# A chunk-selecting attention with a gated MLP: a new held order of the work, the first tile's bounds left out, the bias turned in half or full height

## The chip, the cores and the metric

One core of a Trainium2 chip runs the whole program. The metric is the device time of the run in microseconds, as the median of several runs. The engines are named as in the profile: PE is TensorE (its weight loads are PEld), DVE is VectorE, ACT is ScalarE, POOL is GpSimd, SP is SyncE, which here only issues transfers.

## The reference

Four batches of eight heads, 768 positions, head size 64. Each query picks six chunks of 32 keys by an upper bound of its scores, attends to those alone, and the result goes through a gated MLP that also mixes positions.

```python
k_min = np.min(k_chunks, axis=3)
k_max = np.max(k_chunks, axis=3)
ub = np.sum(np.maximum(q[:, :, :, None, :] * k_min[:, :, None, :, :], q[:, :, :, None, :] * k_max[:, :, None, :, :]), axis=-1)
causal = pos[:, None] // chunk >= np.arange(nc)[None, :]
ub = np.where(causal, ub, -1000000000.0)
top_chunks = np.argsort(ub, axis=-1)[..., -top_k:]
scores = scale * np.matmul(q, k.transpose(0, 1, 3, 2))
sel = (j_chunk == top_chunks[..., None]).any(axis=-2)
mask = sel & (pos[:, None] >= pos[None, :])
scores = np.where(mask, scores, -1000000000.0)
...
attn = attn / (np.sum(attn, axis=-1, keepdims=True) + 1e-09)
return np.matmul(attn, v).astype(np.float32)
...
h = np.maximum(x @ w_in, 0.0)
u, v = (h[..., :d_ff // 2], h[..., d_ff // 2:])
v_n = (v - mu) / np.sqrt(var + 1e-06)
v_s = np.einsum('ts,bsd->btd', w_spatial, v_n) + b_spatial[None, :, None]
gated = u * v_s
return (gated @ w_out).astype(np.float32)
```

## The kernel before

**Tiling.** Heads go in pairs: sixteen pairs `p`, four to a batch `b`. The two heads of a pair lie in partitions 0 to 63 and 64 to 127, so that a product over the head size is a matmul of half height (64 rows, "64*128" in the profile), one for each head; products over 128 rows are of full height ("128*128"). The 768 positions are six tiles `i` of 128, with four chunks each.

**Pieces.** `work_list` cuts the work into 1395 named pieces, each with an engine (or a choice of two), a duration that a planner assumes, the pieces that it comes after, and the buffers that it makes and uses. Pieces of one engine run in the order in which they are written out; between engines semaphores hold them back. For a pair they are, in the order of their data:

| piece | engine | what it does | line |
|---|---|---|---|
| load, cast | SP, POOL | q, k, v from memory; to 16 bits | L633, L621, L638 |
| turn, kT, qT, qp | PE or SP; ACT or DVE | q and k transposed; the negative part of q | L652, L617, L688, L690 |
| ext | DVE | largest and smallest key of each chunk | L671 |
| bounds, ub | PE; ACT or DVE | the upper bounds by matmul; copied out of PSUM | L702; L617, L619, L711 |
| top, leave | DVE | the eight largest bounds of tiles 1 to 5; which chunks are left out | L715, L724 |
| pk, mx | PE, DVE | scores of a unit of keys; their maxima by chunk | L732, L735, L786; L807 |
| minus, kept, shift | POOL, POOL, DVE | the maximum over the chunks that are kept | L811, L817, L824 |
| turn_bias, bT | PE, ACT | the 16-bit bias of every query and chunk, transposed by a matmul with the identity | L831, L835 |
| probs, ex, cut | PE, ACT, POOL | scores again with the bias added; exp; the diagonal cut | L856, L863; L871; L877 |
| weigh, av, sum, inv, norm | PE, ACT, DVE, DVE, POOL or DVE | times v, and divided by the sums | L885, L889, L893, L900, L907 |
| turn_x, xT | PE and ACT, or SP | transposed for the MLP | L922, L931 |

For a batch the MLP's pieces are hv, vr, bn, rstd, vn (one half, normalized), hu, uT (the other half), mix (positions mixed), ms, plus, gT (bias, gate), og, oe, od (the last product, its eviction, its store). They start when a batch's four pairs are done; pieces of pairs of the next batch run among them. The first three pairs find their maxima in another way (kd, fd, fr, fi, fb, L795 and L801).

Small constants are made at the start: `ident`, `far`, `rows` (the four instructions L580 to L585 on POOL, after DVE's `clear`) and `member`, which probs needs.

**First tile.** The queries of tile 0 see at most four chunks, so all visible ones are kept: `top` has no piece for tile 0, its threshold is a constant, and a chunk is left out only where the bound is a huge negative number. `bounds` nevertheless computes all of tile 0. For pairs 0 to 5 (`EARLY`) a matmul of `far` with `big` adds this huge negative number to chunks ahead of the query; for later pairs `ub` adds `far32` on VectorE.

**Order.** Two texts hold the plan: `RANK`, a rank for each piece, and `WHERE`, a letter for each of the 96 pieces that have a choice of engine. `order` runs through a model of the five engines in time: whenever an engine is free it begins the ready piece of lowest rank that finds its buffers free, taking the first buffer that is free in the model. The times of that model come from the durations in `work_list`, 0.095 us for a change between half and full height among them (the kinds in `TILED` are of half height), and a delay after each engine's work. The tile buffers in PSUM are called "two" (three of them) and "mg" (two).

Of the kernel before, what the change touches and what calls it, by code (L numbers as in the profile page):

```python
# [16 lines left out]
P = 128  # L17
# [14 lines left out]
RANK = """  # L32
# [51 lines left out]
"""  # L84
WHERE = """
AAAAGAGAGVGVGAAVAGAGAGVVAGAGAGAVVVVVAVAVAAAAAVVAVGGGGVGGAAVAAAAAAAAAAAVVAVAVVAAVAAVVGGGGGVVAAAAA
"""


class Work:  # L90
# [23 lines left out]
    def order(self):  # L114
# [5 lines left out]
        for i, (_, _, _, after, new, old, _) in enumerate(pieces):  # L120
            for b in new + old:
                users[b] = users.get(b, 0) + 1
            for a in after:
                then[self.index[a]].append(i)
                todo[i] += 1
# [27 lines left out]
        def begin(e):  # L153
            nonlocal bus, late, tiled
            aside, found = [], False
            while ready[e] and not found:
                due, i = heapq.heappop(ready[e])
                if begun[i]:
                    continue
# [907 lines left out]
```

## Time and profile before

| | us |
|---|---|
| median of three runs | 249.05 (248.89 to 249.26) |
| the profiled execution, its time | 248.22 |
| its span, first to last instruction | 246.5 |
| TensorE's granted clock | 1.000 |

The view of waits shows who waited for whom (engine and line, what it waited for: us in total, times, longest). The longest ones of PE and DVE:

```profile
PE mg L652 <- DVE k L619: 6.1, 1, 6.1
DVE tmp L1012 <- PE mg L1001: 7.7, 9, 2.0
DVE rc L893 <- ACT av L889: 4.9, 3, 2.2
PE two L856 <- ACT bT L835: 1.9, 3, 0.8
PE two L856 <- DVE cmax L807: 1.9, 3, 1.0
```

A row of a timeline has the start in us from the span's start, the length, the engine, line, operation, what it writes and reads, and the number of instructions merged into the row; in brackets stands the idle time ahead of it and what ended it. A row of a group has the count, the busy time in us, the mean length of one in ns, and the idle time ahead with those who ended it. Neighbouring instructions of one engine overlap by a little in these rows, as the next starts before the last has drained.

### The profile page before, as it was taken

What the parts mean: (1) busy time and instruction counts of PE and PEld (TensorE: products, weight loads), DVE (VectorE), ACT (ScalarE), POOL (GpSimd) and SP (SyncE); (2) the same over time, 40 slices, a digit from 0 to 9 for tenths busy, and PEclk for the clock granted to TensorE, in tenths of its full rate; (3) what the DMA queues carried; (4) which work ended last, traced back from release to release, by engine and by line L of the source; (5) the groups of instructions that cost most, each with busy time, mean ns of one, the idle gap of its engine ahead of it and who ended that gap; (6) DMA issues with size and microseconds to landing.
All of it is one profiled execution on the core that took longest, in us unless ns stands there. A gap on an engine that the chain in (4) does not pass through costs nothing.

```text
span 246.5 us, 9019 instructions
## 1 busy us (share of the span) xinstructions
PE 224.9 (91%) x3780; PEld 144.6 (59%) x3780; DVE 206.5 (84%) x512; ACT 191.9 (78%) x298; POOL 165.9 (67%) x209
## 2 busy tenths in 40 slices
PE   0898778878999999999999999999999999999993
PEld 0656457666755675666665576666745566645551
DVE  4799999999999999799998997899998853349670
ACT  3598887979998999587859897897679969767312
POOL 8879749887785377999965929999926147402160
PEclk9999999999999999999999999999999999999999
DMA  7969996699999949484899997128900010350005
GB/s 189 325 186 201 257 242 127 122 164 241 168 186 235 216 82 187 89 170 112 190 161 271 175 200 125 34 75 140 268 22 19 0 36 0 105 188 0 0 28 227
DMA packets 93895, 35.51 MB, mean 144 GB/s; under 512 B 86208, under 2 KB 90144, under 8 KB 93856
## 3 DMA queue, kind: packets, MB, share of 16 engines
q1 hardware_dynamic: 91568, 31.81, 61.9%
q0 software_dynamic: 2016, 2.75, 6.5%
q8 instruction: 29, 0.48, 0.8%
q10 hardware_dynamic: 272, 0.39, 0.5%
q14 instruction: 10, 0.08, 0.1%
HBM read 24.77 MB, written 6.29 MB: 126 GB/s over the span
## 4 chain that ended last, share of the span: by engine, by line
PE 48%; DVE 28%; ACT 14%; DMA 4%; issue 3%; POOL 2%; DVEq 0%; ACTq 0%
DVE cmax L807 11%; PE mg L1001 11%; ACT pr L871 8%; PE mg L1024 6%; PE mg L885 5%; PE two L856 4%; PE mg L937 3%; PE two L863 3%; DVE stats L954 3%; DVE ext L671 3%; PE two L786 3%; DVE top L715 2%; PE mg L990 2%; DMA k<-in_k_dram 2%; DVE cmax L801 2%
## 5 line engine op out<-in xcount | busy, mean ns | idle before, releaser
L871 ACT ACTIVATE pr<-two 128x1024 f16<-128x1024 f32 (+1 forms) x96 | 85.3, 934 | 5.4 <-PE two L863 4.8
L807 DVE TENSOR_REDUCE cmax<-two 128x24 f32<-128x768 f32 (+4 forms) x104 | 85.3, 843 | 3.5 <-PE two L735 2.0
L856 PE MATMUL two<-qT,kT 64*128 64x128 f16 (+3 forms) x384 | 40.5, 258 | 5.4 <-ACT bT L835 1.9
L863 PE MATMUL two<-bT,member 64*128 64x128 f16 (+1 forms) x512 | 39.7, 233 | 0.0
L877 POOL TENSOR_SCALAR_AFFINE_SELECT pr<-pr 128x768 f16<-128x768 f16 x32 | 27.9, 886 | 9.1 <-ACT pr L871 9.0
L1019 POOL TENSOR_TENSOR vr<-tmp,uT 128x384 f16<-128x384 f32 x27 | 24.5, 922 | 11.9 <-DVE tmp L1012 11.8
L671 DVE TENSOR_REDUCE ext<-kT 128x24 f16<-128x768 f16 x32 | 29.5, 936 | 1.9 <-ACT kT L617 1.7
L1001 PE MATMUL mg<-wsT,vn 128*128 128x384 f16 x168 | 30.2, 327 | 0.0
L856 PEld LDWEIGHTS <-kT 64*128 64x128 f16 x384 | 19.9, 94 | 17.2 <-issue 15.1
L863 PEld LDWEIGHTS <-member 64*128 64x128 f16 x512 | 25.7, 94 | 5.1
L885 PE MATMUL mg<-v,pr 128*128 128x65 f16 x672 | 25.9, 194 | 0.7 <-POOL pr L877 0.5
L786 PE MATMUL two<-kT,qT 64*128 64x384 f16 (+4 forms) x182 | 24.6, 280 | 1.4 <-ACT pr L871 0.5
L885 PEld LDWEIGHTS <-pr 128*128 128x128 f16 x672 | 23.1, 98 | 3.6 <-issue 1.0
L1001 PEld LDWEIGHTS <-vn 128*128 128x128 f16 x192 | 17.7, 98 | 12.2 <-issue 0.6
L990 PE MATMUL mg<-xT,w_in_sb 128*128 128x384 f16 x112 | 22.4, 328 | 0.0
L907 POOL TENSOR_TENSOR x<-av,rc 128x768 f16<-128x768 f32 x11 | 16.2, 1469 | 8.8 <-DVE rc L900 4.9
L732 PE MATMUL two<-kT,qT 64*128 64x128 f16 x192 | 19.6, 221 | 2.3 <-ACT qT L617 1.0
L1024 PE MATMUL mg<-w_out_sb,vr 128*128 128x512 f16 x84 | 20.8, 380 | 0.0
L937 PE MATMUL mg<-w_in_sb,xT 128*128 128x512 f16 x84 | 20.3, 380 | 0.4 <-DVE o L619 0.4
L889 ACT COPY av<-mg 128x390 f32<-128x390 f32 x32 | 15.6, 500 | 6.2 <-PE mg L885 6.0
L954 DVE BATCH_NORM_STATS2 stats<-vr 128x6 f32<-128x512 f32 x24 | 16.6, 692 | 4.0 <-ACT vr L942 2.9
L735 PE MATMUL two<-half_ahead,ident 64*128 64x64 f16 x192 | 19.8, 193 | 0.0
(113 smaller groups left out, 496.8 us busy)
## 6 DMA issues: line engine op xcount, KB each, us to landing
q<-in_q_dram SPq DMA_DIRECT2D x16, 384.0 KB, 6.4
v<-in_v_dram SPq DMA_DIRECT2D x16, 384.0 KB, 5.7
out_dram<-o SPq DMA_DIRECT2D x24, 256.0 KB, 2.1
k<-in_k_dram SPq DMA_DIRECT2D x15, 384.0 KB, 5.7
vr<-in_moe_w_spatial_dram POOLq DMA_DIRECT2D x6, 192.0 KB, 5.6
w_in_sb<-in_moe_w_in_dram POOLq DMA_DIRECT2D x4, 256.0 KB, 8.8
w_out_sb<-in_moe_w_out_dram POOLq DMA_DIRECT2D x4, 128.0 KB, 4.5
k<-in_k_dram ACTq DMA_DIRECT2D x1, 384.0 KB, 4.7
```

The lines of the kernel that those rows point to most:

```text
L671: nc.vector.tensor_reduce(held["ext", p][:, m], src, axis=AX.X, op=Alu.min if m else Alu.max, negate=(m == 1))
L786: mm(t[:, h, o:o + before], lhsT=qT[rows[h], c], rhs=kT[rows[h], a * CH:a * CH + before], start=True, stop=True)
L807: nc.vector.tensor_reduce(tops(p)[:, i // 2, :, i % 2, a:z], held["two", (p, u)][:, :, o:o + n].rearrange("p h (c e) -> p h c e", e=CH), a ...
L856: mm(t[:, h, z:z + n * P], lhsT=kT[rows[h], keys], rhs=qT[rows[h], i * P:(i + n) * P], start=True, stop=False)
L863: mm(d, lhsT=member[rows[h], r, keys], rhs=bT[rows[h], m * P:(m + w_) * P].rearrange("c (m s) -> c m s", s=P), start=False, stop=(n == 1 o ...
L871: nc.scalar.activation(out=held["pr", p][:, :, c0:c0 + n], in_=held["two", (p, "e", c0)][:, :, 0:n], func=Act.Exp, scale=scale)
L877: nc.gpsimd.affine_select(out=d, in_=d, compare_op=Alu.is_ge, fill=0.0, base=0, channel_multiplier=-1, pattern=[[0, NT], [1, P]])
L885: mm(a[:, i, :], lhsT=pr[:, at[t, i]:at[t, i] + P], rhs=vp[:, h * NT + t, :], start=(t == 0), stop=(t == i))
L937: mm(t, lhsT=held["xT", b][:, ko, i * P:(i + 1) * P], rhs=w_in_sb[:, ko, DH:2 * DH], start=(ko == 0), stop=(ko == NDO - 1))
L990: mm(t, lhsT=w_in_sb[:, ko, db * P:(db + 1) * P], rhs=held["xT", b][:, ko, s * HS:(s + 1) * HS], start=(ko == 0), stop=(ko == NDO - 1))
L1001: mm(t, lhsT=held["vn", b][:, si, db * P:(db + 1) * P], rhs=wsT[:, si, s * HS:(s + 1) * HS], start=(si == 0), stop=(si == NT - 1))
L1024: mm(t, lhsT=held["vr", ("g", b)][:, ko, i * P:(i + 1) * P], rhs=w_out_sb[:, ko, :], start=(ko == 0), stop=(ko == KO - 1))
```

## The change

**The order.** `RANK` and `WHERE` are new. `order` no longer runs a model in time: the rank of a piece is its place in the program. A buffer is taken when its last user has been written out, the one first whose last use lies furthest back. The assumed durations of bounds, norm, bn, rstd1, plus and gT are altered; since the order is held, they no longer enter into it.

```diff
-        free = {e: 0.0 for e in self.ENGINES}
-        ready = {e: [] for e in self.ENGINES}
...
-        heapq.heapify(events)
-        while len(result) < n:
...
+        held = {tag: [None] * k for tag, k in self.bufs.items()}
...
+        for (name, on, _, _, _, _, _), at in zip(pieces, rank):
+            result[at] = name, engine[next(where)] if len(on) > 1 else next(iter(on)), at
+        done = set()
+        for at, (name, _, _) in enumerate(result):
+            _, _, _, after, new, old, _ = pieces[self.index[name]]
+            assert all(a in done for a in after) and all(b in slot for b in old), name
+            for b in new:
+                tenants = held[b[0]]
+                free = [(-1 if x is None else last[x], k) for k, x in enumerate(tenants) if x is None or users[x] == 0]
+                assert free, name
+                slot[b] = min(free)[1]
+                tenants[slot[b]] = b
+            for b in new + old:
+                users[b] -= 1
+                last[b] = at
+            done.add(name)
         return result, slot
```

What the new texts say, read piece by piece against the old order (the ranks begin as follows, 1395 of them):

```diff
 RANK = """
-0 9 100 7 13 10 5 1 28 103 118 168 128 124 256 303 296 313 298 327 425 450 446 421 430 435 398 407 417 422 403 411 388
...
 WHERE = """
-AAAAGAGAGVGVGAAVAGAGAGVVAGAGAGAVVVVVAVAVAAAAAVVAVGGGGVGGAAVAAAAAAAAAAAAVVAVAVVAAVAAVVGGGGGVVAAAAA
+VAAAGVGAGAGAGAAVAVAVAGAVAGAVAGAGAVAGAAAAAAAAVAVAGVGGVVVGAAAVAAAAAAAAAAAAVAAVAVVAAAVGGGVGGGVAAAVVA
```

- 34 of the 96 choices go to another engine. To DVE: kT of pair 0, ub 1, norm 6, 7 and 11, four gT, and some of oe, vn and uT; away from it: ub 3 and 4 and qp 9, 14 and 15 to ACT, norm 13 and 15 and three gT to POOL, and some of oe, vn and uT. In numbers DVE has one kT, one norm and one gT more, and three qp, one oe and one ub fewer.
- About half of each engine's pieces change their place against the others. `rows` on POOL stands behind the casts of k and q 1, k 2 and kd 0, and ahead of the cast of q 2. The loads of v come later on SP, those of q 1 and k 1 earlier.
- On PE half and full height alternate 172 times in the old order and 158 times in the new one; up to turn_bias of pair 4, 33 and 37 times.
- On DVE, shift of pair 11 stands behind ext 13, mx 12.6 and 13.0, 13.1, 13.6 and 13.7, the first four top of pair 13, ub 13, and sum, inv and norm of pair 9, all of which came after it. Shift of pairs 8 and 13 moves ahead.
- On POOL both cuts of pair 15 stand ahead of three gT of batch 2. On ACT the last exp of pair 15 stands behind av 14.1. Turn_x of pair 15 stands ahead of the last og of batch 2.

**The first tile's bounds.** Tile 0 has the matmul of `far` with `big` alone, now for every pair; later pairs get `far32` added as well, which leaves a number as far below the limit.

```diff
-            each = [(big, far[:, i])] * (p < EARLY) + [(qT[:, c], x[:, 0]), (qp[:, c], x[:, 0]), (qp[:, c], x[:, 1])]
+            each = [(big, far[:, i])] * (p < EARLY or i == 0) + [(qT[:, c], x[:, 0]), (qp[:, c], x[:, 0]), (qp[:, c], x[:, 1])] * (i > 0)
```

Each matmul is issued for two heads: 48 become 42 for a pair below 6, and 36 become 32 for the others.

**The turned bias.** Where neither neighbour of a turn_bias on PE is of half height (pairs 5, 9, 10 and 15 in the new order), it is turned over all 128 rows, with the half of the identity that picks the wanted columns. The result is the same.

```diff
+    EITHER = ("turn_bias",)
...
+    turned = [name for name, e, _ in order if e == "PE"]
+    whole = {name[1] for a, name, z in zip(turned, turned[1:], turned[2:])
+             if name[0] in Work.EITHER and not (a[0] in Work.TILED or z[0] in Work.TILED)}
...
-                r = slice(g * D, (g + 1) * D)
-                mm(t[:, g, m * D:(m + 1) * D], lhsT=bias[slot["bias", p]][r, 4 * m:4 * m + 4, :].rearrange("p g c -> p (g c)"), rhs=ident[r, r], start=True, stop=True)
+                r, c = slice(g * D, (g + 1) * D), slice(0, P)
+                if p in whole:
+                    r, c = c, r
+                mm(t[:, g, m * D:(m + 1) * D], lhsT=bias[slot["bias", p]][r, 4 * m:4 * m + 4, :].rearrange("p g c -> p (g c)"),
+                   rhs=ident[r, c] if p in whole else ident[r, r], start=True, stop=True)
```

More of the change, by code (lines that the diff above doesn't have):

```diff
@@ L1 @@
-import heapq
 import math
@@ L32 @@
 RANK = """
[51 rows of a table removed]
[51 rows of a table added]
 """
 WHERE = """
-AAAAGAGAGVGVGAAVAGAGAGVVAGAGAGAVVVVVAVAVAAAAAVVAVGGGGVGGAAVAAAAAAAAAAAVVAVAVVAAVAAVVGGGGGVVAAAAA
+VAAAGVGAGAGAGAAVAVAVAGAVAGAVAGAGAVAGAAAAAAAAVAVAGVGGVVVGAAAVAAAAAAAAVAAVAVAAVVAAAVGGGVGGGVAAAVVA
 """
@@ L116, in order @@
         pieces, n = self.pieces, len(self.pieces)
-        users, slot, freed_at, done_at = {}, {}, {}, {}
-        slots = {tag: [None] * k for tag, k in self.bufs.items()}
-        then, todo, ready_at, begun = [[] for _ in range(n)], [0] * n, [0.0] * n, [False] * n
-        for i, (_, _, _, after, new, old, _) in enumerate(pieces):
+        rank, where = [int(x) for x in RANK.split()], iter(WHERE.replace("\n", ""))
+        engine = dict(P="PE", V="DVE", A="ACT", G="POOL", S="SP")
+        assert sorted(rank) == list(range(n))
@@ L121, in order @@
+        users, slot, last, result = {}, {}, {}, [None] * n
+        held = {tag: [None] * k for tag, k in self.bufs.items()}
+        for _, _, _, _, new, old, _ in pieces:
             for b in new + old:
                 users[b] = users.get(b, 0) + 1
-            for a in after:
-                then[self.index[a]].append(i)
-                todo[i] += 1
-        rank, where = [int(x) for x in RANK.split()], iter(WHERE.replace("\n", ""))
-        engine = dict(P="PE", V="DVE", A="ACT", G="POOL", S="SP")
@@ L318, in work_list @@
         far_pe = p < EARLY
-        add("bounds", {"PE": (6 * far_pe + 18) * 0.027},
+        add("bounds", {"PE": 0.54 if far_pe else 0.412},
             DUE["bounds"],
@@ L396, in work_list @@
                 add("inv", {"DVE": 0.14}, at, 0, after=[("sum", p, 0)], old=[("rc", (p, 0))])
-                add("norm", {"POOL": 1.6, "DVE": 1.45}, at, 0, after=[("inv", p, 0)], old=[("av", p), ("rc", (p, 0))], new=[("x", p)])
+                add("norm", {"POOL": 1.5, "DVE": 1.15}, at, 0, after=[("inv", p, 0)], old=[("av", p), ("rc", (p, 0))], new=[("x", p)])
                 continue
```

87 lines of the change are left out of this document (4 added, 83 removed), and 101 rows, old and new, of the table RANK.

## The prediction

> **What bounds the kernel now.** I began with the page's busy times and chain of waits, then cut the span into three stretches.
>
> ```profile
> span 246.5 us, 9019 instructions
> PE 224.9 (91%) x3780; PEld 144.6 (59%) x3780; DVE 206.5 (84%) x512; ACT 191.9 (78%) x298; POOL 165.9 (67%) x209
> PE 48%; DVE 28%; ACT 14%; DMA 4%; issue 3%; POOL 2%; DVEq 0%; ACTq 0%
> ...
> 0.00:60.00 60.00, 44.91 (x1086) 33.23 (x1087) 54.00 (x154) 47.70 (x66) 47.56 (x76) 1.00 0.92 204
> 60.00:180.00 120.00, 118.30 (x2098) 76.44 (x2097) 112.59 (x274) 100.46 (x162) 95.23 (x110) 1.00 0.88 162
> 180.00:246.50 66.50, 61.71 (x599) 34.92 (x597) 39.86 (x87) 43.72 (x72) 23.09 (x24) 1.00 0.17 57
> ```
>
> The window rows give PE, PEld, DVE, ACT and POOL in that order. Up to 60 us PE is idle for 60 − 44.91 = 15.1 us: there VectorE, busy for 54.00 of 60, hands out the work. From 60 to 180 us PE is idle for only 1.7 us, while VectorE is idle for 7.4 us.
>
> ```profile
> 241.88 0.88 PE two L1024 x4
> 242.82 0.59 ACT o L617
> ```
>
> These two rows of the chain of waits show where PE ends: 241.88 + 0.88 = 242.8 us. After it come 3.7 us of eviction and store, so of PE's 4.8 idle us after 180 about 1.1 lie ahead of its end. From 60 us on PE waits about 2.8 us in all. A microsecond of PE work taken out behind 60 us therefore shortens the run, unless PE then waits for something else; taken out ahead of 60 us it only widens a gap.
>
> **The change part by part.** First the prices, in three stretches of PE's timeline (start, length, operation).
>
> ```profile
> 101.96 0.20 PE L702 MATMUL two<-ext,qp 64*128 64x24 f16 x4
> ...
> 102.33 0.20 PE L702 MATMUL two<-ext,qp 64*128 64x24 f16 x4
> ...
> 127.29 1.03 PE L937 MATMUL mg<-w_in_sb,xT 128*128 128x512 f16 x4
> 128.25 0.26 PE L831 MATMUL two<-ident,bias 64*128 64x64 f16 x6
> 128.44 0.39 PE L937 MATMUL mg<-w_in_sb,xT 128*128 128x512 f16 x1
> ...
> 211.87 1.02 PE L1024 MATMUL mg<-w_out_sb,vr 128*128 128x512 f16 x4
> 212.73 0.83 PE L885 MATMUL mg<-v,pr 128*128 128x65 f16 x21
> ```
>
> *First tile's bounds.* Between the two L702 rows lie five tiles of six matmuls: 0.37 us / 30 = 12.3 ns each. The edit drops 6 matmuls for each of pairs 0 to 5 and 4 for each of pairs 6 to 15. The first 36 (0.44 us) mostly fall in the stretch where PE has gaps, so I count them as nothing; without that cover they would be worth 0.44. The other 40 are worth 40 × 12.3 ns = **0.49 us**.
>
> *Changes of height.* From og to weigh, both of full height, the next start lies 211.87 + 1.02 − 212.73 = 0.16 us ahead of the end before it. From hv to the half-height turned bias it lies 127.29 + 1.03 − 128.25 = 0.07 ahead, and back again 128.25 + 0.26 − 128.44 = 0.07. A change of height thus costs about 0.095 us (0.16 − 0.07, at the rows' two digits). Walking PE's pieces in the two held orders I count 172 changes before and 158 after, 8 of those removed by the turned bias in full height. Up to turn_bias of pair 4 (59.7 us in the trace) there are 33 before and 37 after; behind it 139 and 121. Behind it 18 × 0.095 = **1.71 us** go; the four added ahead of it (0.38 us) lie in PE's gaps.
>
> *Turned bias in full height.* This meets pairs 5, 9, 10 and 15. Six half-height matmuls start (0.26 − 0.19) / 5 = 14 ns apart, taking the 0.19 us of one matmul as the last one's length. Its nearest full-height row is weigh: (0.83 − 0.19) / 20 = 32 ns. So the piece grows by 5 × 18 = 0.09 us, four times: **−0.36 us**. Bounds: nothing, if its passes overlapped as before, and 0.36.
>
> The Trainium skill, "TensorEngine Tiling (Array Packing)", speaks on both sides. Its "Key Properties" say that a change of tiling mode drains TensorE, and the 0.095 us at L831 agrees. Its "When to Use Tiling" advises two row tiles for a contraction of 64, up to twice as fast, which this edit gives up. By a plain doubling of the 0.07 us of starts the four would lose an estimated 0.28 instead of 0.36.
>
> So PE's work behind 60 us falls by 0.49 + 1.71 − 0.36 = **1.84 us**. Two small pk pieces also move ahead of turn_bias 4; I count that as nothing, since the early stretch may pay for it.
>
> *The engines of 34 pieces and the moved orders.* VectorE's durations, from the groups of instructions (count, then busy us, mean ns):
>
> ```profile
> L807 DVE TENSOR_REDUCE cmax<-two 128x24 f32<-128x768 f32 (+4 forms) x104 | 85.3, 843 | 3.5 <-PE two L735 2.0 <-PE two L786 1.3
> L671 DVE TENSOR_REDUCE ext<-kT 128x24 f16<-128x768 f16 x32 | 29.5, 936 | 1.9 <-ACT kT L617 1.7
> L907 POOL TENSOR_TENSOR x<-av,rc 128x768 f16<-128x768 f32 x11 | 16.2, 1469 | 8.8 <-DVE rc L900 4.9 <-ACT bT L835 3.3 <-ACT pr L871 0.3
> L907 DVE TENSOR_TENSOR x<-av,rc 128x768 f16<-128x768 f32 x5 | 5.0, 996 | 0.1
> L715 DVE MAX8 top<-ub 128x8 f32<-128x16 f32 (+4 forms) x160 | 14.8, 156 | 0.0
> L711 DVE TENSOR_TENSOR ub<-two,far 128x288 f32<-128x288 f32 x10 | 4.4, 441 | 2.5 <-PE two L702 2.4
> L619 DVE COPY o<-mg 128x512 f32<-128x512 f32 x6 | 4.1, 678 | 3.4 <-PE mg L1024 3.4
> L1019 DVE TENSOR_TENSOR vr<-tmp,uT 128x384 f16<-128x384 f32 x5 | 3.6, 739 | 0.2
> L690 DVE TENSOR_SCALAR qp<-qT 128x768 f16<-128x768 f16 x3 | 1.3, 424 | 0.2 <-DMA qT<-q 0.2
> L619 DVE COPY ub<-two 128x288 f32<-128x288 f32 x2 | 0.9, 446 | 0.0
> ...
> 3.86 0.73 POOL L580 MEMSET member<- 32x768 f16 x1
> ...
> 6.82 0.73 POOL L585 MEMSET member<- 1x768 f16 x1
> ```
>
> VectorE gains one norm (+0.99), one gT (+0.74) and kT 0 (about 0.8, in its idle time ahead of the first ext). It loses three qp (1.27), one oe (0.68) and one ub (0.45). The balance is +0.1, or −0.7 without kT 0: **nothing**, with PE's work as the cover. GpSimd loses a norm and a gT. ScalarE gains the three qp, an oe and a ub and gives up kT 0; at 78% it has room. The moved loads, casts and `rows` go past other pieces of SP's and GpSimd's queues: `rows` (the last two lines, 3.86 to 7.55: 3.7 us at GpSimd's start) now stands ahead of the cast of q 2. GpSimd is idle for 12.4 of the first 60 us, so I take nothing; if the early stretch lacked that cover it could lose up to those 3.7.
>
> *VectorE's waits for GpSimd.* A "leave" (L724), its two group rows, two long ones, and GpSimd beside the second:
>
> ```profile
> L724 DVE SCALAR_TENSOR_TENSOR bias<-top,ub x16: 442/502/1164, 14.0 to 188.4; 128x288 f16<-128x288 f32 x16
> L724 DVE SCALAR_TENSOR_TENSOR bias<-top,ub 128x288 f16<-128x288 f32 x16 | 10.3, 646 | 0.1
> 28.44 1.04 DVE L724 SCALAR_TENSOR_TENSOR bias<-top,ub 128x288 f16<-128x288 f32 x1
> ...
> 40.38 1.06 DVE L724 SCALAR_TENSOR_TENSOR bias<-top,ub 128x288 f16<-128x288 f32 x1
> 39.44 1.68 POOL L877 TENSOR_SCALAR_AFFINE_SELECT pr<-pr 128x768 f16<-128x768 f16 x2
> 41.08 1.04 POOL L638 CAST v<-v 128x768 f16<-128x768 f32 x1
> L638 POOL CAST v<-v 128x768 f16<-128x768 f32 x16 | 13.6, 852 | 0.2
> ```
>
> At 40.38 it takes 1.06 us where the shortest takes 0.44, ending 0.3 us after GpSimd's cut; the next cast then takes 1.04 instead of 0.85. Over 16 the excess is 10.3 − 16 × 0.442 = 3.2 us, the most that a better order could regain here; the other bound is as much again, if the new order meets GpSimd more often. I take zero: where the overlaps fall is set at run time, and PE binds where most of them lie.
>
> The Trainium skill's "SBUF — State Buffer", "Who interferes with whom", says that a VectorE instruction with two SBUF inputs and a GpSimd one that reads SBUF exclude each other for a whole instruction. This case's rows agree. By it a wait avoided on VectorE can reappear on GpSimd, so a full 3.2 us off the sum would be too much.
>
> *New waits.* The turned bias of a pair waits for `shift` (L824), and everything on PE stands behind it.
>
> ```profile
> 147.34 0.45 DVE L824 TENSOR_REDUCE bias<-kept 128x12 f16<-128x288 f32 x1
> 155.89 0.25 PE L831 MATMUL two<-ident,bias 64*128 64x64 f16 x6
> ```
>
> For pair 11 the slack is 155.89 − 147.79 = 8.1 us. In the new order five mx, one ext, four top, norm, sum and inv of pair 9, ub 13, two moved norms and ub 1 come ahead of shift 11, and two oe, one qp and two ub leave. By the means above, with 0.38 for sum and inv, that is 4.2 + 0.9 + 0.6 + 3.0 + 0.4 + 0.9 − 2.7 = 7.3 us. PE meanwhile reaches turn_bias 11 about 0.9 us of work sooner. The slack left is 8.1 − 7.3 − 0.9, about nothing. I charge **+0.4 us** for waits there, between none and the rival below.
>
> *The tail.*
>
> ```profile
> 211.52 2.49 POOL L877 TENSOR_SCALAR_AFFINE_SELECT pr<-pr 128x768 f16<-128x768 f16 x2 [2.65 <-ACT pr L871]
> 214.06 0.84 PE L885 MATMUL mg<-v,pr 128*128 128x65 f16 x21 [0.50 <-POOL pr L877]
> 219.15 0.81 PE L937 MATMUL mg<-w_in_sb,xT 128*128 128x512 f16 x3 [0.45 <-DVE o L619]
> ```
>
> PE waits 0.50 us for pair 15's second cut. The new order makes both cuts before three gT pieces, and weigh 15.0 waits instead for the last exp, which og 2.3 and 2.0 (about 1.7 us) nearly cover: **−0.4 us**. Norm 15 moves to GpSimd (1469 against 996 ns), but turn_x 15 now stands ahead of the last og: the 0.45 us stays.
>
> **Sum.** −1.84 + 0.4 − 0.4 = −1.84. The profiled execution took 248.22 us (its span and 1.72 around it) and would take 246.4. The median of the runs, 249.05, lies 0.83 above it; I forecast **247.2 us**.
>
> **Rivals.**
>
> *VectorE gains too (0.18).* The leaves at 28.44 and 40.38 lose 0.6 us each in the stretch where PE waits for VectorE. Without these waits and without the late ones: 249.05 − 1.84 − 1.2 − 0.4 = 245.6. For it: VectorE's 54.00 of 60. Against: by the means above, shift 3 and 4 now stand behind 0.4 and 1.5 us more VectorE work.
>
> *Late shifts, slower (0.27).* In the stretch 60 to 180 VectorE's 7.4 us of idle grow by 40%, or 3.0 us, because its order is more tightly bound to PE, ScalarE and the three "two" buffers. With no slack at pairs 9 to 11, PE stops for it: 249.05 − 1.84 + 3.0 + 0.2 = 250.4. It decides once VectorE is over 1.84 us later there than planned. Against: at p 8 and 13 shift moves ahead.
>
> *Even (0.13).* The same lateness, about 1.8 us: 249.05. The work goes, and PE waits instead.
>
> **How the numbers follow.** The forecast has 0.42. About 0.2% or 0.5 us separates a change from none, so faster means under 248.55: 0.18 and nearly all of 0.42 give 0.60; same 0.13; slower 0.27. The range 245.3 to 250.3 leaves out the upper half of the slow rival (0.13) and the far third of the first (0.06). The forecast's own range is 246.4 (no late waits, and the early bounds' 0.44 counted) to 248.2 (no gain in the tail, and one more long leave among the early ones, 0.6).
>
> **What would show it.** The bounds should show 76 matmuls fewer. PE's starts across a height change stay 0.095 us dearer. PE idle between 60 us and its end should stay at 2 to 4 us; 5 or more, with turn_bias behind L824, is the slower rival. If L724's mean falls near 450 ns and PE's idle before 60 us under 14 us, the first rival holds. The prediction is wrong if PE's early idle grows by over 1.5 us.

## The result, and the profile after

The changed kernel takes **257.18 us** (median of 4 runs, 256.91 to 258.07) against 249.16 for the kernel before beside it: a ratio of 1.0328, with a 95% interval from 1.0300 to 1.0356. The forecast was 247.2 us with a range from 245.3 to 250.3. Both the sign and the range were wrong.

The page of the changed kernel (its span is 256.4 us), busy times and the shares of its chain of waits; then its windows (PE, PEld, DVE, ACT, POOL busy, granted clock, DMA share, GB/s):

```profile
PE 227.2 (89%) x3704; PEld 147.0 (57%) x3704; DVE 214.5 (84%) x510; ACT 194.9 (76%) x302; POOL 165.2 (64%) x207
DVE 41%; PE 40%; ACT 7%; DMA 6%; POOL 4%; issue 1%; DVEq 0%; ACTq 0%; POOLq 0%
...
0.00:60.00 60.00, 44.35 (x1008) 32.69 (x1008) 54.33 (x150) 45.78 (x64) 45.42 (x74) 0.97 0.89 193
60.00:180.00 120.00, 110.96 (x1909) 72.55 (x1908) 111.59 (x250) 97.23 (x156) 86.26 (x100) 0.96 0.84 147
180.00:256.40 76.40, 71.86 (x797) 41.75 (x793) 48.56 (x112) 51.91 (x83) 33.48 (x34) 1.00 0.35 83
...
60.00:80.00 20.00, 16.75 (x303) 12.09 (x301) 16.10 (x37) 15.24 (x23) 11.04 (x15) 0.91 0.91 147
80.00:100.00 20.00, 15.78 (x289) 10.87 (x286) 19.45 (x38) 15.03 (x26) 9.76 (x13) 0.89 1.20 198
...
20.33:23.72 3.39, 3.39 (x26) 1.79 (x24) 3.39 (x8) 3.07 (x5) 1.86 (x3) 0.50 0.53 122
```

The same two short stretches of the kernel before:

```profile
60.00:80.00 20.00, 19.78 (x310) 12.65 (x308) 19.18 (x42) 18.18 (x29) 14.32 (x19) 1.00 1.20 201
80.00:100.00 20.00, 19.72 (x381) 13.20 (x378) 19.40 (x53) 19.09 (x32) 12.84 (x14) 1.00 0.92 164
```

The span grew by 9.9 us. PE's idle time makes 7.65 of it (29.2 − 21.6): +0.56 before 60 us, **+3.03 from 60 to 80, +3.94 from 80 to 100**, +0.37 from there to 180, −0.25 behind. PE's busy time makes the other 2.25, though it issues 76 matmuls fewer: the granted clock is 0.91 and 0.89 in the same two stretches, 0.94 from 100 to 120 us and 0.50 from 20.3 to 23.7 us, where it was 1.00, so matmuls last longer. The chain of waits, 48% PE and 28% DVE before, is now 40% PE and 41% DVE. So nearly all of the added idle time lies between 60 and 100 us. This is the timeline there, with two later rows of PE (start, length, engine; in brackets what ended the wait):

```profile
61.74 0.40 PE L538 MATMUL mg<-ident,vr 128*128 128x128 f16 x4
63.77 0.23 PE L538 MATMUL mg<-ident,vr 128*128 128x128 f16 x1 [1.64 <-DMA vr<-in_moe_w_spatial_dram]
64.85 0.29 PE L538 MATMUL mg<-ident,vr 128*128 128x128 f16 x1 [0.85 <-DMA vr<-in_moe_w_spatial_dram]
...
91.10 0.58 POOL L533 DMA_DIRECT2D w_out_sb<-in_moe_w_out_dram  x1
91.31 4.36 DVE L905 SCALAR_TENSOR_TENSOR nmr<-mv,rstd 128x6 f32<-128x6 f32 x1
91.69 0.84 POOL L567 CAST v<-v 128x768 f16<-128x768 f32 x1
92.47 0.87 POOL L809 TENSOR_SCALAR_AFFINE_SELECT pr<-pr 128x768 f16<-128x768 f16 x1
93.29 0.82 POOL L567 CAST v<-v 128x768 f16<-128x768 f32 x1
94.06 0.82 POOL L550 CAST q<-q 128x768 f16<-128x768 f32 x1
94.83 0.82 POOL L550 CAST k<-k 128x768 f16<-128x768 f32 x1
97.28 0.20 PE L631 MATMUL two<-far,big 64*128 64x24 f16 x2 [4.22 <-DVE ub L640]
...
136.40 0.35 PE L762 MATMUL two<-ident,bias 128*128 128x64 f16 x6 [0.58 <-DVE cmax L736]
```

Two things are new. Turn_ws (L538) of tile 4 now stands ahead of the weights' arrival, and PE waits 1.64 + 0.85 us for the transfer. And `nmr`, the product of rstd2 (L905), 128 x 6 numbers, takes **4.36 us**: it starts at 91.31 and ends at 95.67, with the last of five instructions that GpSimd runs without a pause (94.83 + 0.82 = 95.65). Everything behind it on VectorE waits, so the `ub` that frees a "two" buffer comes late, and PE stands 4.22 us ahead of bounds 8. In the kernel before the same product met GpSimd's cuts at the same place of its order:

```profile
85.22 1.69 POOL L877 TENSOR_SCALAR_AFFINE_SELECT pr<-pr 128x768 f16<-128x768 f16 x2
85.38 0.72 DVE L973 SCALAR_TENSOR_TENSOR nmr<-mv,rstd 128x6 f32<-128x6 f32 x1
```

There it ended at 86.10, between the two cuts. Two groups of VectorE's instructions that read two operands from SBUF, after:

```profile
L653 DVE SCALAR_TENSOR_TENSOR bias<-top,ub 128x288 f16<-128x288 f32 x16 | 12.0, 763 | 0.0
L905 DVE SCALAR_TENSOR_TENSOR nmr<-mv,rstd 128x6 f32<-128x6 f32 (+1 forms) x5 | 6.1, 1214 | 0.1
```

Before, the leaves took 10.3 us and the five `nmr` 1.3: these are 1.7 and 4.8 us more. The new order meets more of these waits, not fewer.

### The profile page after: what moved, and what is told of

Read it like the earlier page. It is cut to its first block, busy times and chain, and to the rows that moved or that the text cites. A ratio compares the mean times of both kernels' runs of the same rounds, so it can differ in the third digit from the quotient of the medians.

```text
span 256.4 us, 8826 instructions
## 1 busy us (share of the span) xinstructions
PE 227.2 (89%) x3704; PEld 147.0 (57%) x3704; DVE 214.5 (84%) x510; ACT 194.9 (76%) x302; POOL 165.2 (64%) x207
## 4 chain that ended last, share of the span: by engine, by line
DVE 41%; PE 40%; ACT 7%; DMA 6%; POOL 4%; issue 1%; DVEq 0%; ACTq 0%; POOLq 0%
DVE cmax L736 16%; PE mg L933 9%; PE mg L956 5%; DVE ext L600 5%; PE mg L817 5%; DVE stats L886 4%; DMA vr<-in_moe_w_spatial_dram 4%; PE two L788 3%; DVE bias L653 3%; ACT pr L803 3%; PE two L795 3%; DVE top L644 2%; DVE nmr L905 2%; PE two L715 2%; PE mg L922 2%; DMA k<-in_k_dram 2%
## 5 line engine op out<-in xcount | busy, mean ns | idle before, releaser
L736 DVE TENSOR_REDUCE cmax<-two 128x24 f32<-128x768 f32 (+4 forms) x104 | 85.0, 844 | 7.3 <-PE two L664 4.0
L809 POOL TENSOR_SCALAR_AFFINE_SELECT pr<-pr 128x768 f16<-128x768 f16 x32 | 30.1, 948 | 10.9 <-ACT pr L803 10.7
L933 PE MATMUL mg<-wsT,vn 128*128 128x384 f16 x168 | 30.9, 327 | 0.1
L788 PEld LDWEIGHTS <-kT 64*128 64x128 f16 x384 | 19.5, 94 | 16.1 <-issue 13.7
L817 PE MATMUL mg<-v,pr 128*128 128x65 f16 x672 | 27.6, 198 | 0.0
L715 PE MATMUL two<-kT,qT 64*128 64x256 f16 (+4 forms) x182 | 25.6, 287 | 1.9 <-DVE cmax L736 1.4
L817 PEld LDWEIGHTS <-pr 128*128 128x128 f16 x672 | 24.6, 101 | 3.5 <-issue 1.0
L839 POOL TENSOR_TENSOR x<-av,rc 128x768 f16<-128x768 f32 x10 | 14.7, 1472 | 16.2 <-DVE rc L832 14.9
L661 PE MATMUL two<-kT,qT 64*128 64x128 f16 x192 | 20.2, 225 | 2.3 <-ACT qT L546 0.9
L922 PE MATMUL mg<-xT,w_in_sb 128*128 128x384 f16 x112 | 21.8, 327 | 0.2
L664 PE MATMUL two<-half_ahead,ident 64*128 64x64 f16 x192 | 20.4, 195 | 0.0
L869 PE MATMUL mg<-w_in_sb,xT 128*128 128x512 f16 x84 | 20.3, 380 | 0.0
L912 ACT ACTIVATE vn<-vr,nmr,rstd 128x512 f16<-128x512 f32 x21 | 16.4, 811 | 5.0 <-DVE nmr L905 5.0
```

Of the source, the lines that this page charges most:

```text
L715: mm(t[:, h, o:o + before], lhsT=qT[rows[h], c], rhs=kT[rows[h], a * CH:a * CH + before], start=True, stop=True)
L736: nc.vector.tensor_reduce(tops(p)[:, i // 2, :, i % 2, a:z], held["two", (p, u)][:, :, o:o + n].rearrange("p h (c e) -> p h c e", e=CH), a ...
L788: mm(t[:, h, z:z + n * P], lhsT=kT[rows[h], keys], rhs=qT[rows[h], i * P:(i + n) * P], start=True, stop=False)
L809: nc.gpsimd.affine_select(out=d, in_=d, compare_op=Alu.is_ge, fill=0.0, base=0, channel_multiplier=-1, pattern=[[0, NT], [1, P]])
L817: mm(a[:, i, :], lhsT=pr[:, at[t, i]:at[t, i] + P], rhs=vp[:, h * NT + t, :], start=(t == 0), stop=(t == i))
L922: mm(t, lhsT=w_in_sb[:, ko, db * P:(db + 1) * P], rhs=held["xT", b][:, ko, s * HS:(s + 1) * HS], start=(ko == 0), stop=(ko == NDO - 1))
```

## Experiments

Each ratio is against runs of the kernel before on the same chip (their medians were 248.3 to 248.8 us), with its 95% interval.

### The product of rstd2

**a2_nmr_gpsimd: the product is made by GpSimd itself, behind its power; VectorE only turns the mean's sign.**

```diff
         mv, rstd, nmr, _ = held["part", b, g]
         nc.vector.tensor_scalar(rstd, in0=mv[:, :, 1], scalar1=1e-6, scalar2=None, op0=Alu.add)
+        nc.vector.tensor_scalar(nmr, in0=mv[:, :, 0], scalar1=-1.0, scalar2=None, op0=Alu.mult)
...
         nc.gpsimd.tensor_tensor(rstd, in0=rstd, in1=minus, op=Alu.pow)
+        nc.gpsimd.tensor_mul(nmr, nmr, rstd)
...
-        nc.vector.scalar_tensor_tensor(nmr, in0=mv[:, :, 0], scalar=-1.0, in1=rstd, op0=Alu.mult, op1=Alu.mult)
```

> The changed kernel with the product of mean and 1/std (nmr, rstd2) on GpSimd, right behind its power, and the sign put on the mean by VectorE ahead of it: VectorE no longer has this instruction with two inputs, which took 4.36 us at 91.3 us beside six GpSimd instructions in a row. Theory 'two late hand-overs': TensorE's wait of 4.2 us at bounds 8 and the halved clock behind it (6.8 us at half speed, up to 3.4 us) come back in part: 257.2 - 4 to 7 = 250 to 253. Rival 'late shifts': VectorE is late through many small waits, and those 4.4 us are slack elsewhere: 255.5 to 257.2.

251.16 us, ratio 1.0095 [1.0064, 1.0126]: 6.0 us less than the changed kernel's 257.18, with everything else of the change in it. The product takes GpSimd about 0.2 us. Windows of a2:

```profile
60.00:80.00 20.00, 17.45 (x261) 12.49 (x261) 15.34 (x35) 14.81 (x23) 10.71 (x14) 0.83 0.84 137
80.00:100.00 20.00, 19.68 (x378) 13.50 (x376) 19.45 (x56) 19.43 (x34) 12.42 (x17) 1.00 1.24 198
```

From 80 to 100 us PE's idle time is back at 0.3 us and the clock at 1.00. From 60 to 80 us 2.55 us of idle time stay, at a granted clock of 0.83. About three quarters of the loss went with this one instruction of VectorE.

**a6_gap: three of the casts moved away, so that GpSimd pauses earlier.** A piece order is edited, here and below, by a list of names that are taken out and put behind another.

```diff
+MOVES = [([('cast', 8, 'v'), ('cast', 10, 'q'), ('cast', 10, 'k')], ('minus', 7))]
...
+        for group, anchor in MOVES:
+            moved = [r for g in group for r in result if r[0] == g]
+            result = [r for r in result if r[0] not in group]
+            at = [r[0] for r in result].index(anchor) + 1
+            result[at:at] = moved
```

> The changed kernel with three of GpSimd's casts (v 8, q 10, k 10) moved from behind cut 5.0 to behind minus 7, which waits for VectorE's leave 7: the unbroken run of GpSimd instructions beside rstd2 0 ends with cut 5.0 at 93.34 us instead of 95.65. Theory 'VectorE gets its second input only when GpSimd pauses': rstd2 0 takes about 2.0 us instead of 4.36, and the run falls by 2.3 to 5 us: 252.2 to 254.9. Rival 'one GpSimd instruction is all that it waits for, the rest is something else': rstd2 0 stays above 4 us, 256.5 to 257.5.

256.45 us, ratio 1.0326 [1.0272, 1.0381].

```profile
90.24 2.06 DVE L913 SCALAR_TENSOR_TENSOR nmr<-mv,rstd 128x6 f32<-128x6 f32 x1
```

The product now ended when the cut ended and GpSimd paused, 2.06 us after it began. So here, too, the wait lasted as long as GpSimd's unbroken run. The time hardly moved: with the casts later, PE stood 1.8 us ahead of a probs of pair 6 for which it had not waited.

**c1_issue: the transfer of weights ahead of the run is moved away.** In the kernel before a cut, not a transfer, follows the power.

```diff
+MOVES = [([('weights', 'out', 2)], ('kept', 7))]
```

> The changed kernel, with GpSimd's third transfer of the output weights moved from right behind the power of rstd1 0 to behind kept 7, so that a cast follows the power. Theory (a transfer that GpSimd issues while VectorE's product of rstd2 0 asks for memory is what lets the casts behind it keep VectorE out): the product takes 0.7 to 1.6 us in place of 4.36, and the time falls by 4 to 6 us to 251 to 253.5. Rival (any casts and a cut in a row are enough): the product stays above 3.5 us and the time at 256 to 258.

255.83 us, ratio 1.0284 [1.0239, 1.0330]. The product did what the theory wanted, and the time did not. Rows of c1's timeline:

```profile
89.99 0.63 DVE L913 SCALAR_TENSOR_TENSOR nmr<-mv,rstd 128x6 f32<-128x6 f32 x1
...
99.38 0.64 POOL L541 DMA_DIRECT2D w_out_sb<-in_moe_w_out_dram  x1
100.05 1.01 POOL L950 TENSOR_TENSOR tmp<-tmp,bB 128x384 f32<-128x384 f32 x1
100.95 3.89 DVE L661 SCALAR_TENSOR_TENSOR bias<-top,ub 128x288 f16<-128x288 f32 x1
101.01 0.87 POOL L817 TENSOR_SCALAR_AFFINE_SELECT pr<-pr 128x768 f16<-128x768 f16 x1
101.85 0.92 POOL L959 TENSOR_TENSOR vr<-tmp,uT 128x384 f16<-128x384 f32 x1
102.72 0.99 POOL L950 TENSOR_TENSOR tmp<-tmp,bB 128x384 f32<-128x384 f32 x1
103.67 0.85 POOL L817 TENSOR_SCALAR_AFFINE_SELECT pr<-pr 128x768 f16<-128x768 f16 x1
106.62 0.19 PE L639 MATMUL two<-far,big 64*128 64x24 f16 x2 [2.93 <-DVE cmax L744]
```

The product got in after one cast of GpSimd (89.78 to 90.60), 0.63 us. Eleven microseconds later a leave (L661) waited through five GpSimd instructions, 3.89 us against 0.44 for a free one, and got in when GpSimd paused at 104.52; PE then waited 2.93 us ahead of bounds 9. **The long wait isn't tied to one instruction.** It came back elsewhere and took most of the gain with it. Whether a transfer ahead of the run has a part in it c1 can't say: the moved transfer itself now stands at the head of this run (99.38).

**b4_run and c2_run_issue: runs of GpSimd made in the kernel before.** Behind the power of rstd1 0 five casts to a tile that nothing reads; in c2 a transfer ahead of them.

```diff
+        if b == 0:
+            nc.gpsimd.dma_start(out=spare2, in_=moe_w_out[0:P, :])
+            for _ in range(5):
+                nc.gpsimd.tensor_copy(spare, bB)
```

(b4 is without the `dma_start` line.)

> The kernel before with five casts of a 128x768 table into a spare tile, which nobody reads, behind GpSimd's power of batch 0 (some 4.1 us of GpSimd work in a row). Theory 'VectorE gets its second input only when GpSimd pauses': the first nmr takes 4 us or more instead of 0.72, and the time grows by 4 to 7 us, 253 to 256. Rival 'it is held back by one instruction at most': the nmr stays near 1 us; what is left is GpSimd's delay, below 2 us.

> The kernel before with, behind the power of rstd1 0 on GpSimd, one transfer of 128 rows of the output weights to a spare tile and then five casts to a spare tile (b4_run had the five casts alone: product 0.67 us, ratio 1.0076). Theory (the transfer issue ahead): the product takes 3.5 to 5 us and the ratio rises to 1.015 to 1.03. Rival: the product stays below 1.7 us and the ratio at 1.005 to 1.012.

b4: 250.38 us, 1.0076 [1.0049, 1.0104]. c2: 250.50 us, 1.0079 [1.0052, 1.0107]. Timelines of b4, then of c2:

```profile
85.31 0.81 POOL L973 CAST spare<-bB 128x768 f16<-128x768 f32 x1
85.48 0.67 DVE L977 SCALAR_TENSOR_TENSOR nmr<-mv,rstd 128x6 f32<-128x6 f32 x1
86.19 0.83 POOL L973 CAST spare<-bB 128x768 f16<-128x768 f32 x1
```

```profile
85.98 0.61 POOL L973 DMA_DIRECT2D spare<-in_moe_w_out_dram  x1
86.16 1.31 DVE L979 SCALAR_TENSOR_TENSOR nmr<-mv,rstd 128x6 f32<-128x6 f32 x1
86.60 4.41 POOL L975 CAST spare<-bB 128x768 f16<-128x768 f32 x5
```

In both the product got in after the first cast. But these runs are not unbroken. The five casts, which all write the same tile, stand 0.06 us apart: in b4 the first ends at 85.31 + 0.81 = 86.12 and the second begins at 86.19, and of the 4.39 us from the first start to the last end GpSimd is busy for 4.14. In the changed kernel each instruction of the run began some 0.05 us before the one ahead had ended (91.69 + 0.84 = 92.53, and the next at 92.47). The product got in at the first pause. So b4 and c2 don't test an unbroken run; c2 shows only that a transfer ahead doesn't carry the wait over such a pause.

A pause isn't always needed: in the kernel before the product at 85.38 got in between two cuts of which the second began (86.05) before the first had ended (86.08). **In all runs a leave or a product that waited got in at the first pause of GpSimd of 0.06 us or more, if not before. When it is let in between two overlapping instructions, and when it is kept out until a pause, stays open.** (The issue of a transfer is no such pause: in the changed kernel and in c2 the product began during one, and wasn't let in.)

**b5_run_nmr: b4 with the product on GpSimd** (a2's edit).

> The same five casts, and nmr on GpSimd ahead of them: GpSimd is delayed as much, VectorE has no nmr. Theory: 0 to 2 us above b2_nmr (248.2), so 248.2 to 250.2. Rival 'GpSimd's delay of its own pieces is the cost': as slow as b4_run.

251.13 us, 1.0104 [1.0076, 1.0132]; with b4 the intervals overlap. So the five casts seem to cost what they cost by holding GpSimd up, not VectorE.

**a4_clock: does the clock matter by itself?** The four matmuls of hu 0.0.1, which stand ahead of the 4.22 us gap, are issued seven times over with the same result, so that PE keeps working.

```diff
-        for ko in range(NDO):
+        for ko in list(range(NDO)) * (7 if (b, db, s) == (0, 0, 1) else 1):
```

> The changed kernel with the four matmuls of hu 0.0.1 issued seven times instead of once (the same result each time): 6 x 0.65 = 3.9 us of TensorE work that lies in the 4.2 us in which it waits ahead of bounds 8, and should keep its clock up there. Theory 'the clock is a cost of its own': the half clock from 95.4 to 102.2 us goes or shrinks to one period of 3.4 us, and 1.7 to 3.4 us come back: 253.8 to 255.5. Rival 'the wait alone': behind the wait VectorE's lateness sets the pace, and at most 0.5 us comes back: 256.7 to 257.4.

256.19 us, 1.0296 [1.0249, 1.0342]. The granted clock from 80 to 100 us was 1.00 instead of 0.89, and the time about 0.8 us lower by the ratios, with overlapping intervals (from 60 to 80 us a4's clock was lower, 0.83 for 0.91). The lost clock behind that gap is worth something like a microsecond, not more closely resolved; the wait itself is the bulk.

### What is left: the order from 60 to 80 us, or the order behind

**a1_ws_later and a3_both: turn_ws moved behind the transfer**, in the changed kernel and in a2.

```diff
+MOVES = [([('turn_ws', 4), ('turn_ws', 3), ('wsT', 4), ('wsT', 3), ('turn_ws', 5), ('turn_ws', 2), ('wsT', 5), ('wsT', 2), ('turn_ws', 1), ('wsT', 1)], ('ex', 4, 2048))]
```

> The changed kernel with five of the six transposes of the spatial weights (turn_ws 4, 3, 5, 2, 1 and their evictions wsT) moved on TensorE and ScalarE behind probs 4.512 and ex 4.2048, the last transfer of these weights having landed at 64.8 us in the changed kernel's trace. Theory 'two late hand-overs': the 2.5 us that TensorE waited for that transfer and most of what the halved clock from 64.7 to 68.1 us cost (up to 1.7 us) come back: 257.2 - 3 to 4.5 = 252.7 to 254.2. Rival 'late shifts': the turned biases of pairs 5 and 6 stand behind VectorE anyway, so that at most 0.5 us comes back: 256.7 to 257.4.

> Both edits. Theory 'two late hand-overs': 257.2 - 7 to 10.5 = 246.5 to 250, the changed kernel then being at or below the kernel before. Rival 'late shifts': 254 or more.

a1: 256.96 us, 1.0318 [1.0277, 1.0359], no gain, and `nmr` still takes 4.36 us. a3: 250.21 us, 1.0068 [1.0053, 1.0083], some 0.7 us under a2 by the ratios, within the overlap of the two intervals. The window of a3:

```profile
60.00:80.00 20.00, 16.38 (x286) 11.45 (x285) 16.81 (x36) 15.82 (x26) 11.25 (x15) 1.00 0.98 147
```

PE's wait for the transfer was gone and PE idle 3.6 us there all the same; VectorE is idle for 3.2 too. The stretch has no single latecomer.

**a5_spread, a8_shift4, c5_load7: other single moves with the product on GpSimd.** a5 spreads turn_ws and wsT over five later places; a8 is a3 with shift 4 put behind inv 2; c5 is a3 with the load of the spatial bias put behind that of k 8.

```diff
+MOVES = [([('turn_ws', 4), ('wsT', 4)], ('ex', 4, 2048)), ([('turn_ws', 3), ('wsT', 3)], ('ex', 4, 512)), ([('turn_ws', 5), ('wsT', 5)], ('pk', 6, 3)), ([('turn_ws', 2), ('wsT', 2)], ('xT', 3)), ([('turn_ws', 1), ('wsT', 1)], ('wsT', 0))]
...
+MOVES = [..., ([('shift', 4)], ('inv', 2, 0))]
...
+MOVES = [..., ([('b_load',)], ('load', 8, 'k'))]
```

> The changed kernel with nmr on GpSimd and with five transposes of the spatial weights spread one by one behind ex 4.2048, ex 4.512, pk 6.3, xT 3 and wsT 0, instead of in a block (a3_both, 250.2). Theory: the block itself held pk 5.3 back, VectorE waited 3.0 us for it, and TensorE's waits from 60 to 80 us were still 5.65 us against 1.09 before; spread out, 2 to 3.5 us come back: 246.7 to 248.2. Rival 'VectorE's order is late there in any case' (shift 5 and 6 stand behind more VectorE work): 249.5 to 250.5.

> The kernel of a3_both (250.2) with shift of pair 4 moved ahead on VectorE, behind inv 2, past two top, two ext and one mx. In a3_both turn_bias 4 ran at 60.4 us against 59.7 before, and TensorE then waited 5.65 us from 60 to 80. Theory 'VectorE's order makes the early stretch late' (the prediction charged nothing for the 1.5 us more work ahead of shift 4): turn_bias 4 comes at 58 to 59, and 1 to 2.5 us come back: 247.7 to 249.2. Rival 'TensorE's own order from 60 to 80 is what waits' (the fill work of the MLP begins 4 us later, behind turn_x 3): 249.8 to 250.6.

> a3_both (250.21 us) with the transfer of the spatial bias on SP's queue moved from ahead of the loads of q 7 and k 7 to behind the load of k 8. In a3_both GpSimd stands 3.65 us at the cast of k 7 for its transfer, and TensorE loses 5.65 us from 60 to 80 us. Theory (the late loads of pair 7 hold GpSimd, VectorE and then TensorE): the wait falls under 1.5 us, TensorE loses 2 to 3 us less there, 247 to 248.5 us. Rival (the order of TensorE and VectorE is late there by itself): 249.7 to 250.5 us.

a5: 251.05 us, 1.0095 [1.0060, 1.0131]. a8: 251.33 us, 1.0117 [1.0089, 1.0144]. c5: 251.14 us, 1.0105 [1.0074, 1.0137]; GpSimd's wait for k 7 is only 0.7 us shorter in it. None of the three is faster than a3, and all three theories fell. (The 5.65 us that the expectations give for TensorE from 60 to 80 us is more than its idle time in a3's window, 3.62 us.)

**h1_late and h2_early: the two orders cut and joined.** All pieces up to the second half of weigh 4 in the order and on the engines of one kernel, all others as in the other kernel; both have the two small edits and a2's product. Only the texts of ranks and engines differ.

```diff
 RANK = """
...
 WHERE = """
...
```

> Order and engines of the kernel before for all pieces up to the second half of weigh 4 (82.5 us), the changed kernel's order and engines for all the rest; bounds left out, turned bias in either height (pairs 1, 6, 9, 10, 15 in full), and the product of rstd2 on GpSimd as in a2_nmr_gpsimd. Behind that point TensorE changes height 102 times in place of 110, makes 40 fewer bounds matmuls and turns three biases in full height: by the prediction's terms -0.76 - 0.49 + 0.27 = -1.0 us. Theory (what is left of the loss comes from the order of the first 85 us): TensorE loses about 1 us from 60 to 80 us as before, and the time is 0 to 1.2 us under that of the kernel before. Rival (the later order waits as well): 1 to 3 us over the kernel before.

> The other way round: the changed kernel's order and engines up to the second half of weigh 4 (89.6 us in its trace), those of the kernel before for the rest; the same edits and the product of rstd2 on GpSimd. Theory (the early order holds the rest of the loss): TensorE loses 4 to 6 us from 60 to 80 us, and the time is 2 to 4 us over the kernel before (a2_nmr_gpsimd: 2.4 over). Rival (the later order holds it): within 1 us of the kernel before.

h1, with the old order first: 248.98 us, **1.0027** [1.0007, 1.0046]. h2, with the new order first: 253.14 us, **1.0167** [1.0121, 1.0213]. Window of h1:

```profile
60.00:80.00 20.00, 19.81 (x310) 12.91 (x306) 19.34 (x41) 17.92 (x29) 14.02 (x19) 1.00 1.25 201
```

Window of h2:

```profile
60.00:80.00 20.00, 16.33 (x266) 11.43 (x261) 15.44 (x36) 14.45 (x23) 10.40 (x15) 0.91 0.90 143
```

The new order of the first 85 us brings the idle stretch from 60 to 80 us with either order behind it (3.67 us in h2, 2.55 in a2); the old one does not (0.19 in h1). That places most of what is left in the early order, though not in one piece of it. The run h2 lies 4.8 us over the kernel before by the medians, where a2, with the same early order and its own late one, lies 2.4 over. The other 2.4 us may come from joining two orders that were not made for each other; the runs don't show it.

The run h1 says what the late part of the change is worth alone: it was expected 0 to 1.2 us under the kernel before, and its interval lies 0.2 to 1.1 us over it. So its theory held for the stretch and failed for the time. The expected 1.0 us less of PE's work can't be seen in its profile: from 60 us on PE is busy 0.29 us less than before (179.72 for 180.01) and idle 0.69 us more (7.18 for 6.49), but b2 below, whose PE work is unchanged, shows 0.18 less and 0.88 more in the same comparison.

### The work taken out

**b1_bounds, b2_nmr, b3_edits: the kernel before with the first tile's bounds left out; with a2's product; with both and the turned bias in either height** (its order has five such pairs, 1, 6, 9, 13 and 14).

```diff
-            each = [(big, far[:, i])] * (p < EARLY) + [(qT[:, c], x[:, 0]), (qp[:, c], x[:, 0]), (qp[:, c], x[:, 1])]
+            each = [(big, far[:, i])] * (p < EARLY or i == 0) + [(qT[:, c], x[:, 0]), (qp[:, c], x[:, 0]), (qp[:, c], x[:, 1])] * (i > 0)
```

> The kernel before, its order unchanged, with the first tile's bounds left out alone. By the prediction's term: 40 matmuls behind 60 us at 12.3 ns, 0.49 us, less what VectorE takes back: 248.3 to 249.0. Rival: TensorE's queue is not what binds, no change: 249.0 to 249.3.

> The kernel before, its order unchanged, with nmr on GpSimd alone. In its trace the first nmr took 0.72 us and the others 0.13 to 0.17. Theory 'two late hand-overs': there is nothing to regain here, 248.2 to 249.1. Rival 'nmr on VectorE is a cost in itself, whatever the order': 246 or less.

> The kernel before in its own order, with nmr on GpSimd, the first tile's bounds left out and the bias turned in full height for the five pairs (1, 6, 9, 13, 14) whose neighbours allow it: all that the change and the experiments brought except the new order. By the prediction's terms 0.49 us of bounds and 5 x (2 x 0.095 - 0.09) = 0.5 us of turned bias, 0.5 us measured for nmr: 247.2 to 248.2. Rival, since the bounds alone changed nothing: 248.0 to 248.7.

b1: 249.06 us, 1.0017 [0.9998, 1.0037]. b2: 248.24 us, 0.9981 [0.9963, 1.0000]. b3: 248.21 us, 0.9990 [0.9971, 1.0009]. None can be told from the kernel before; b2 is the best that the runs found. By the prediction's terms b1 and b3 should have been faster, and neither can be shown to be.

**a9_half: a3 with every turned bias at half height again.**

```diff
-             if name[0] in Work.EITHER and not (a[0] in Work.TILED or z[0] in Work.TILED)}
+             if name[0] in () and not (a[0] in Work.TILED or z[0] in Work.TILED)}
```

> a3_both (250.21 us) with every turned bias at half height as before, the order kept: four pieces return to 0.26 us and bring eight changes of height back. By the prediction's terms 8 x 0.095 - 0.36 = +0.4 us: 250.4 to 250.9 us. Rival (TensorE's waits take up what is gained, as with the bounds): no change, 250.0 to 250.4 us.

251.13 us, 1.0103 [1.0050, 1.0156] against a3's 1.0068 [1.0053, 1.0083]. The difference of 0.9 us has the sign that the terms give, but the intervals overlap: inconclusive.

## Why the prediction was wrong

**The step that failed: VectorE's waits for GpSimd at zero, between −3.2 and +3.2 us.** They grew by 6.5 us, 1.7 in the leaves and 4.8 in `nmr`. The bound came from the sixteen leaves alone. It left out `nmr`, which reads two operands from SBUF as well and whose row stood in the trace at 0.72 us. And it took the excess of the old order, doubled, for the most that could come, although a leave of the kernel before, a row that the working didn't show, had already waited past the end of one GpSimd instruction:

```profile
105.37 0.85 POOL L877 TENSOR_SCALAR_AFFINE_SELECT pr<-pr 128x768 f16<-128x768 f16 x1
106.16 1.16 DVE L724 SCALAR_TENSOR_TENSOR bias<-top,ub 128x288 f16<-128x288 f32 x1
106.19 0.81 POOL L621 CAST q<-q 128x768 f16<-128x768 f32 x1
```

It waited through the last 0.06 us of a cut and the whole cast behind it, with no transfer ahead. In the changed kernel one product waited through five instructions, 4.36 us. The cover that was named ("PE binds where most of them lie") was gone at once: with VectorE busy 19.4 of 20 us beside PE's 19.7 from 80 to 100 us, a stall of VectorE became a stall of PE, here 4.22 us of it. Taking the product off VectorE gave 6.0 of the 10.0 us between forecast and result back (a2). Shortening the wait alone did not: in a6 and c1 other waits took its place.

The Trainium skill, "SBUF — State Buffer", "Who interferes with whom", says that a VectorE instruction with two SBUF inputs contends with a GpSimd instruction that reads SBUF. Of the ports that the two engines share it says, for VectorE's two-port modes, that the first to issue has them "for the whole instruction". The trace agrees that a small product can be shut out entirely, and shows that one instruction is not the limit: five passed here and in c1, two in a6.

**Moved pieces at nothing.** The forecast gave the moved loads, casts and the early order no cost, with GpSimd's 12.4 idle us as cover and at most 3.7 us of loss ahead of 60 us. Idle time before 60 us grew by 0.56 only, so that cover held. But the cost came just behind, from 60 to 80 us, which the working took for a stretch where PE cannot starve: turn_ws was moved ahead of its transfer (2.5 us), and with that mended other waits took the place (a3, 3.6 us). h1 and h2 put the idle stretch on the early order as a whole. The working looked at each queue's idle time; what was missing was each moved PE piece against the landing of its data: turn_ws began at 61.74 us instead of 63.5, while the last of its transfers landed at 64.8 instead of 61.3. Which piece of the early order costs the rest stays open.

**The granted clock at 1.00 throughout.** The forecast did not ask what a new gap does to the clock. The profile of the changed kernel shows half the clock from 64.7 to 68.1 and from 95.4 to 102.2 us, behind the waits of 1.64 + 0.85 and of 4.22 us, and from 20.3 to 23.7 us, where no wait in the 5 us ahead is over 0.74 us. PE's busy time grew by 2.25 us with less work. The Trainium skill, "TensorE: Matmul & The Clock Gate", "The HAM clock gate", has a drop to half after an idle window of about 3.4 us. The gap of 4.2 us agrees, and a4, which filled it, kept 1.00 from 80 to 100 us. Behind the shorter waits the clock fell all the same, yet behind c1's single wait of 2.93 us it stayed at 1.00 (100 to 120 us): these runs give no length of wait that decides.

**PE's work, −1.84 us: its prices held, its worth did not.** The matmuls are 76 fewer (3780 to 3704). The full-height turned bias takes 0.35 us (136.40) for 0.26, the +0.09 predicted. A change of height still costs the same, by the tail of the changed kernel:

```profile
219.76 0.38 PE L795 MATMUL two<-bT,member 64*128 64x256 f16 x4
220.07 1.50 PE L817 MATMUL mg<-v,pr 128*128 128x65 f16 x42
...
223.29 1.58 PE L817 MATMUL mg<-v,pr 128*128 128x65 f16 x42
...
229.02 1.89 PE L869 MATMUL mg<-w_in_sb,xT 128*128 128x512 f16 x8
230.75 1.89 PE L869 MATMUL two<-w_in_sb,xT 128*128 128x512 f16 x8
```

Across a change the overlap is 219.76 + 0.38 − 220.07 = 0.07 us, without one 229.02 + 1.89 − 230.75 = 0.16. The sum itself can't be read from the busy times, with the clock lower. But "a microsecond of PE work taken out behind 60 us shortens the run, unless PE then waits for something else" met its exception each time: the intervals of b1 and h1 leave out the 0.49 and 1.0 us that the terms give them, and b3's leaves out the 1.5 that its expectation adds up. That PE waited for VectorE instead is the likely reason; the profiles are too coarse to show it.

**The tail, −0.4 us: right.** The two halves of weigh 15 run as one group (223.29, x42) with no wait between them, where the second waited 0.50 us before; and the 0.45 us ahead of the last batch's first hv, which the forecast left in, is gone as well (229.02 follows the og at once). Both are real and lost in the rest.

**New waits at the turned bias, +0.4 us: near in size, by luck.** Pair 11's turned bias, for which it was charged, doesn't wait. PE waits 0.58 us ahead of pair 9's (136.40), and what ends that wait is an mx (L736), not a shift.

**The rivals.** The slower one (250.4) had the direction and its mark in the profile, over 5 us of PE idle behind 60 us (9.0 up to 180 us alone, for 1.7 before), but not the mechanism: VectorE's idle from 60 to 180 grew from 7.4 to 8.4 us, not to 10.4, and the turned bias is not where PE waits. "VectorE gains too" fell with the leaves' mean, 763 ns for 646.

## What to carry to other kernels

Where one engine can shut another out, the worst wait to reckon with is the neighbour's whole unbroken run, up to its next pause, not one instruction of it: look for small two-operand instructions of VectorE that everything else queues behind, and put them on the engine that makes their operand. Where two engines are both some 97% busy, don't count on work taken from one of them: here it bought nothing that could be measured. And check each piece that a new order moves forward against the landing time of its own data, in a stretch that has no slack first of all.

## What the runs showed of the hardware

The wait of a VectorE instruction for GpSimd isn't bounded by one GpSimd instruction: 4.36 us and 3.89 us through five that overlapped, ended by GpSimd's pause. A pause of 0.06 us is enough to get in (0.67 us in front of five casts in b4). Between overlapping instructions VectorE was let in at some places (0.72 us at 85.38 in the kernel before) and not at others; what decides this was not found. The third of the changed kernel's 128 x 6 products, let in at once, took 0.15 us. The granted clock fell to half for 3.4 to 6.8 us, behind one wait of PE of 4.22 us, behind two of 1.64 and 0.85, and once where none was over 0.74; behind one of 2.93 us in c1 it stayed full.
